# Hash attention and a feed-forward block on one core: hashes taken two pairs ahead, transposes and normalization change places

## The chip, the cores and the metric

The kernel runs on one core of one Trainium2 chip. The metric is the time of the device in microseconds (us), the median of several runs. "PE" is TensorE (PEld its weight loads), "DVE" VectorE, "ACT" ScalarE, "POOL" GpSimd, "SP" SyncE; SPq is SyncE's queue of DMA issues. L432 is line 432 of the kernel.

## What is computed

```python
batch, n_heads, seq, head_dim = (4, 8, 768, 64)           # q, k, v; proj is 64 x 6
q_bits = (np.einsum('bhsd,dk->bhsk', q, proj) > 0)         # the same for k
q_bucket = np.sum(q_bits * powers, axis=-1)                # powers = 1, 2, 4, ... 32
mask = q_bucket[:, :, :, None] == k_bucket[:, :, None, :]
scores = scale * np.matmul(q, k.transpose(0, 1, 3, 2))
scores = np.where(mask, scores, -1000000000.0)
...
attn = np.exp(scores - max) / (sum + 1e-09)
out = np.matmul(attn, v)
# rows of all heads side by side: x is 3072 x 512
h = x @ w_in                                               # 512 x 2048
g = h * (1.0 / (1.0 + np.exp(-1.702 * h)))
y = g @ w_out                                              # 2048 x 512
```

A query sees only the keys whose six hash bits are the same as its own.

## The kernel before

**Pairs of heads.** Attention runs over 16 pairs of heads (`pairs`, L144): two heads of 64 dimensions fill 128 partitions. Pair 0 has a path of its own (`first_pair`), and the loop at L553 takes the pairs 1 to 15. For each pair the kernel needs the keys and the queries turned, so that the dimension lies on the partitions (kT, qT), and a "feature" tile of each (kf, qf), made from the hash bits: the product of features adds a large negative number to each score whose bits differ, so no mask is needed.

**Steps of a pair n**, as functions:
- `fetch` (L317) loads keys or queries, four DMAs of 96 KB each; one buffer for each of the two names. `fetch_v` (L330) loads the values, two DMAs of 192 KB, two buffers.
- `turn` (L388): DVE's transpose L391 of keys or of queries; kT and qT have two buffers each, so kT of pair n+2 lies where kT of pair n lay. `measure` (L393): ACT's sum of squares L398, for a guard.
- `hashed` (L402): PE's matmuls L408 into one bank of PSUM (tag "m"), all four at once in four groups of 32 columns. `featured` (L411): DVE compares the hashes L413 into f (one buffer), and eight small DMAs L420 carry f into the feature tiles, of which there are two sets, for even and odd pairs.
- `scores` (L423): a "phase" for each half c of the queries. For each of six tiles of keys PE adds the product of features and that of keys and queries (L432) into a score tile (pool `sps`, three tiles of two banks), and ACT takes the exponential (L433). The phase with c = 0 is called that on rows, that with c = 1 that on columns.
- `add_low` (L437): POOL adds the first three tiles of exponentials (L440, L441). `add_high` (L443): DVE adds the other three and POOL's sum (L446, L448).
- `values` (L450): PE multiplies by V (L458); c = 0 goes into the bank of pool `aps`, c = 1 into the bank of pool `mps`, the one that hashes use too. `unload` (L466): ACT moves the result into xT (L469, L470).
- `total` (L472): PE sums over the partitions (dn, L479), again four groups of 32 columns. `invert` (L481): DVE turns the sums, takes reciprocals and turns them back (L485 to L494). `norm` (L497): DVE multiplies xT by them (L499).
- `step` and `begin` (L504, L508): six DVE steps and one ACT step (L178 to L198) that convert a chunk of the first weight matrix, one chunk for each pair from 2 on; ACT's step L190 stands ahead of the second unload of the pair in ACT's order.

**What sets the order.** PE, DVE, ACT and POOL are in `manual_schedule` (L72): they do their instructions in the order of the code. SP isn't in it: the order of its DMA issues is found by the framework's scheduler, and each DMA is issued when SP comes to it and its waits are met. So the code of the loop is PE's, DVE's, ACT's and POOL's programme, and a wait in one of these orders holds up all that stands behind it on that engine.

**In the loop before**, pair n has this order on PE: scores on rows, scores on columns, hash of n+1, values of both halves, sums. On DVE: rt of pair n-1, keys of n+1 turned, reciprocals and rs of n-1, queries of n+1 turned, add_high on rows, f of n+1, normalization of n-1, add_high on columns, conversion. In the last pair a guard (`guard`, L516) stands after add_high on rows: DVE reduces the sizes (L518), PE turns them (row, L521), DVE reduces again (L522).

**Feed-forward.** `feed_forward` (L679) follows, with products by seven-multiplication block schemes for both matrices (`hidden`, L700, PE L708; `product_of_halves`, L809, PE L820). `sums_b` of its input (`x_sums`, L514; L219 to L222 on DVE) is spread over the pairs 12 to 15, one step at the end of each. Its first pool of PSUM banks takes the six banks of `sps`, which is closed before (L596). There is a second, slower path behind the guard (L984), which isn't run with this data.

Of the kernel before, what the change touches and what calls it, by code (L numbers as in the profile page):

```python
# [8 lines left out]
F32 = mybir.dt.float32  # L9
# [10 lines left out]
P = 128  # L20
# [18 lines left out]
def kernel(  # L39
# [28 lines left out]
    HS = HT * P  # L68
# [84 lines left out]
    for x in (0x3FFFFFFF, 0xFF800000):  # L153
        m = const.tile([P, 1], U32, name=f"mask_{x:x}")
# [128 lines left out]
    def attention(ff):  # L283
# [4 lines left out]
        with actx:  # L288
# [28 lines left out]
            def fetch(n, name):  # L317

                b, hp = pairs[n]
                x = raws[n, name] = ld.tile([P, S // 32, 32], F32, tag=name, name=name)  # L320
                if (n, name) == (2, "q"):
                    behind(x[:, 0, 0:1])
                src = {"k": k, "q": q}[name]
                for j in range(2):
                    rows = src[b, 2 * hp + j].rearrange("(s p) (a i) -> a p s i", p=32, i=32)
                    for a in range(D // 32):
                        r0 = D * j + 32 * a
                        loader[0].dma_start(out=x[r0 : r0 + 32], in_=rows[a])
# [59 lines left out]
            def turn(n, name):  # L388
                x = raws[n, name]
                xt = xts[n, name] = wk.tile([P, S], F32, tag=f"{name}T", name=f"{name}T")  # L390
                nc.vector.transpose(xt, x.rearrange("p s i -> p (s i)"))  # L391

            def measure(n, name):  # L393

                x = raws.pop((n, name))
                i = 2 * n + "kq".index(name)
                junk = st.tile([P, S], BF16, tag="junk", name="junk", bufs=1)
                nc.scalar.activation(junk, x.rearrange("p s i -> p (s i)"), Act.Square, accum_out=sizes[:, i : i + 1])  # L398
# [3 lines left out]
            def hashed(n):  # L402

                h = dots[n] = mps.tile([P, HS], F32, tag="m", name="hash")
                for i, x in enumerate("kq"):
                    for c in range(2):
                        r0 = D * i + 32 * c
                        nc.tensor.matmul(h[r0 : r0 + 32, :], pf[x], xts[n, x][:, c * HS : (c + 1) * HS],  # L408
                                         start=True, stop=True)

            def featured(n):  # L411
                f = wk.tile([P, HS], BF16, tag="f", name="f", bufs=1)
                nc.vector.tensor_scalar(f, dots.pop(n), above[:, 0:1], weight[:, 0:1], op0=Alu.is_gt, op1=Alu.mult)  # L413
                for c in range(2):
                    for i, x in enumerate("kq"):

                        queue = nc.scalar if (n, x, c) == (1, "q", 0) else nc.sync
                        for j in range(2):
                            r0 = D * i + 32 * c + 2 * NB * j
                            queue.dma_start(out=feats[n % 2][x][D * j : D * j + 2 * NB, c * HS : (c + 1) * HS],  # L420
                                            in_=f[r0 : r0 + 2 * NB, :])

            def scores(n, c, kts):  # L423
                qT, kT, qf, kf = xts[n, "q"], xts[n, "k"], feats[n % 2]["q"], feats[n % 2]["k"]
                cols = slice(c * HS, (c + 1) * HS)
                for kt in kts:
                    ps = sps.tile([P, 2, 512], F32, tag="s", name="ps")
                    keys = slice(kt * P, (kt + 1) * P)
                    for a, m, last in ((kf, qf, False), (kT, qT, True)):
                        for j in range(2):  # L430
                            hs = slice(D * j, D * (j + 1))
                            nc.tensor.matmul(ps[:, j, 0:HS], a[hs, keys], m[hs, cols], start=not last, stop=last)  # L432
                    nc.scalar.activation(es[c][:, kt, :, 0:HS], ps[:, :, 0:HS], Act.Exp, scale=1.0 / D**0.5)  # L433

            accs, avs = {}, {}
# [14 lines left out]
            def values(n, c, kts):  # L450
                if 0 in kts:

                    pool, tag = (mps, "m") if c else (aps, "av")
                    avs[n, c] = pool.tile([P, HS + 1], F32, tag=tag, name="av")
                av, vt = avs[n, c], vts[n]
                for t in kts:
                    for j in range(2):
                        nc.tensor.matmul(av[D * j : D * (j + 1), :], vt[:, t, j, :], es[c][:, t, j, :],  # L458
                                         start=(t == 0), stop=(t == T - 1))
# [6 lines left out]
            def unload(n, c):  # L466
                av = avs.pop((n, c))
                vs = st.tile([P, 1], F32, tag="vs", name="vs")
                nc.scalar.copy(vs, av[:, HS : HS + 1])  # L469
                nc.scalar.activation(x_of(n)[:, c * GT : (c + 1) * GT, :], av[:, 0:HS].rearrange("p (t s) -> p t s", t=GT), Act.Identity, bias=vs[:, 0:1])  # L470

            def total(n):  # L472

                dn = accs[n] = aps.tile([P, HS], F32, tag="av", name="dn")
                for c in range(2):
                    acc = accs.pop((n, c))
                    for j in range(2):
                        r0 = D * j + 32 * c
                        nc.tensor.matmul(dn[r0 : r0 + 32, :], ones[:, 0:32], acc[:, j, :], start=True, stop=True)  # L479

            def invert(n):  # L481


                rt = st.tile([P, HS // 32, 32], F32, tag="rt", name="rt", bufs=1)
                nc.vector.transpose(rt.rearrange("p s i -> p (s i)"), accs.pop(n))  # L485
                yield
                r = st.tile([P, 2, HS // 32], F32, tag="r", name="r")
                nc.vector.reciprocal(r, rt[:, :, 0].unsqueeze(1).to_broadcast([P, 2, HS // 32]))
                for r0 in range(0, P, 32):
                    c = r0 // 32 % 2  # L490
                    r1 = r0 + 32 - 64 * c
                    nc.vector.reciprocal(r[r1 : r1 + 32, c], rt[r0 : r0 + 32, :, 0])
                rs = accs[n] = st.tile([P, S], F32, tag="rs", name="rs", bufs=1)
                nc.vector.transpose(rs.rearrange("p (s i) -> p s i", i=32),  # L494
                                    r.rearrange("p c s -> p (c s)").unsqueeze(2).to_broadcast([P, S // 32, 32]))

            def norm(n):  # L497
                x, rs = x_of(n), accs.pop(n)
                nc.vector.tensor_tensor(x, x, rs.rearrange("p (t s) -> p t s", t=T), op=Alu.mult)  # L499
# [4 lines left out]
            def step(n, count=1):  # L504
                for _ in range(count):
                    next(conv.get(n, iter(())), None)
# [40 lines left out]
            fetch(2, "q")  # L547
            fetch_v(1)
            scores(0, 1, high)
            values(0, 1, low)  # L550
            values(0, 1, high)
            unload(0, 1)
            for n in range(1, last + 1):  # L553
                scores(n, 0, every)
                add_low(n, 0)
                if n == 1:
                    add_high(0, 1)
                    turn(2, "k")
                    total(0)
                inverted = invert(n - 1)  # L560
                next(inverted)
                if 1 < n < last:
                    turn(n + 1, "k")
                whole(inverted)
                scores(n, 1, every)
                add_low(n, 1)
                if n < last:
                    turn(n + 1, "q")
                add_high(n, 0)
                if n < last:  # L570
                    hashed(n + 1)
                    featured(n + 1)
                    for x in "kq":
                        measure(n + 1, x)
                else:
                    guard(0)
                    guard(1)
                norm(n - 1)
                add_high(n, 1)
                values(n, 0, every)  # L580
                unload(n, 0)
                step(n, 6)
                values(n, 1, every)
                unload(n, 1)
                total(n)
                if n + 2 <= last:
                    for x in "kq":
                        fetch(n + 2, x)
                if n < last:
                    fetch_v(n + 1)  # L590
                    begin(n + 1)
                if n > last - len(x_sums):
                    x_sums[n - last - 1]()
# [378 lines left out]
    def whole(steps):  # L972
        for _ in steps:
            pass
# [46 lines left out]
```

## Time and profile before

| | |
|---|---|
| median of 3 runs | 877.33 us (876.5 to 877.67) |
| profiled execution: time, span | 876.77 us, 875.0 us |
| granted clock of TensorE | 0.997 |
| attention, to the first feed-forward product | 322.8 us |
| a pair from 2 on | 19.28 us (71.11 to 90.39) |

Share of the chain of work that ended last, by line:

```profile
PE 90%; DVE 6%; SPq 1%; DMA 1%; issue 1%; ACT 0%; ACTq 0%; DVEq 0%
```

The page gives busy time by engine and by group of instructions, the timeline the instructions of an engine in order of time. A row of the timeline has the start, the duration, the engine, the line, the operation, the tile that is written and those that are read, and the count; at its end, in brackets, stands the idle time before it and what ended that. Rows of like instructions are merged. A stretch of the span is given with its busy us for each engine, the granted clock, the share of the DMA engines and the GB/s that they moved. For a DMA the row on SPq is that of its issue.

### The profile page before, as it was taken

To read this page: it belongs to the slowest core of one execution; us is meant where nothing else is said; L and a number is where in the kernel's file an instruction comes from. 1 tells how busy PE (TensorE), PEld (TensorE's weight loads), DVE (VectorE), ACT (ScalarE), POOL (GpSimd) and SP (SyncE) were. 2 spreads that over 40 slices of the span, in tenths; PEclk is the share of its full clock that TensorE was granted. 3 is DMA by queue.
4 is the path that set the end of the run, shared out by engine and by line. 5 is a ranking of instruction groups with operands and counts; after the bars stand their busy time and mean duration, and the time that the engine had idled before them with its cause. 6 is when DMAs were issued, how large, how long until landed. Compare 5 with 4: busy or idle time off the path is not lost.

```text
span 875.0 us, 11818 instructions
## 1 busy us (share of the span) xinstructions
PE 861.9 (99%) x4077; PEld 502.7 (57%) x4077; DVE 719.6 (82%) x1020; ACT 310.2 (35%) x519; POOL 321.3 (37%) x275
## 2 busy tenths in 40 slices
PE   9999999999999999999999999999999999999995
PEld 4444445444444444444444444444888888888884
DVE  4579999988999997788777787888888977897785
ACT  5756567777666743222233222332000000000000
POOL 4243334334333475665443344659903100000000
PEclk9999999999999999999999999999999999999998
DMA  5334456644445304555455645575844685467524
GB/s 133 59 59 85 83 97 106 119 87 83 84 83 93 73 25 145 204 205 204 166 188 190 214 168 200 193 251 168 308 160 163 199 244 198 166 203 241 193 97 99
DMA packets 169155, 131.99 MB, mean 151 GB/s; under 512 B 123616, under 2 KB 138112, under 8 KB 163712
## 3 DMA queue, kind: packets, MB, share of 16 engines
q1 hardware_dynamic: 166528, 129.70, 51.5%
q10 hardware_dynamic: 2560, 1.46, 0.7%
q8 instruction: 34, 0.56, 0.3%
q14 instruction: 33, 0.27, 0.1%
HBM read 79.69 MB, written 50.33 MB: 149 GB/s over the span
## 4 chain that ended last, share of the span: by engine, by line
PE 90%; DVE 6%; SPq 1%; DMA 1%; issue 1%; ACT 0%; ACTq 0%; DVEq 0%
PE product L708 33%; PE product L820 27%; PE ps L432 16%; PE av L458 12%; PE dn L479 1%; PE hash L408 1%; DVE acc L448 1%; DVE acc L446 1%; DVE xT L824 1%; SPq L420 1%; DVE y L800 1%; DVE xT L499 1%; DMA pj<-in_proj_dram 0%; DMA k<-in_k_dram 0%; DVE t_x L221 0%
## 5 line engine op out<-in xcount | busy, mean ns | idle before, releaser
L432 PE MATMUL ps<-qT,kT 64*128 64x384 f32 x768 | 155.1, 483 | 0.0
L433 ACT ACTIVATE e<-ps 128x768 f32<-128x768 f32 x192 | 149.0, 813 | 15.7 <-PE ps L432 13.7
L708 PE MATMUL product<-xT,w_in_sb 128*128 128x512 f32 x288 | 135.5, 593 | 0.0
L458 PE MATMUL av<-e,v 128*64 128x385 f32 x768 | 128.2, 488 | 0.0
L440 POOL TENSOR_TENSOR acc<-e 128x768 f32<-128x768 f32 x32 | 50.4, 1575 | 192.2 <-ACT e L433 113.4
L716 ACT ACTIVATE c<-c 128x512 f32<-128x512 f32 x72 | 45.3, 630 | 186.7 <-issue 78.6
L458 PEld LDWEIGHTS av<-e,v 128*64 128x64 f32 x768 | 53.9, 136 | 72.8 <-issue 71.9
L708 PEld LDWEIGHTS product<-xT,w_in_sb 128*128 128x128 f32 x288 | 54.7, 190 | 68.9 <-issue 64.4
L708 PE MATMUL product<-t_x,s_in 128*128 128x512 f32 x192 | 90.3, 592 | 0.0
L432 PEld LDWEIGHTS ps<-qT,kT 64*128 64x128 f32 x768 | 68.3, 188 | 36.1 <-issue 35.2
L219 POOL TENSOR_TENSOR v<-c,u 128x512 f32<-128x512 f32 x24 | 34.2, 1423 | 122.8 <-ACT c L716 122.8
L833 ACT COPY u<-product 128x256 f32<-128x256 f32 x21 | 7.8, 372 | 172.1 <-PE product L820 138.9
L441 POOL TENSOR_TENSOR acc<-acc,e 128x768 f32<-128x768 f32 x32 | 64.1, 2002 | 2.5
L432 PE MATMUL ps<-qf,kf 64*128 64x384 bf16 x384 | 63.1, 324 | 0.1
L708 PEld LDWEIGHTS product<-t_x,s_in 128*128 128x128 f32 x192 | 36.6, 190 | 45.9 <-issue 43.2
L446 DVE SCALAR_TENSOR_TENSOR acc<-e 128x768 f32<-128x768 f32 x32 | 52.1, 1628 | 5.1 <-ACT e L433 5.1
L708 PE MATMUL product<-xT,s_in 128*128 128x512 f32 x96 | 45.1, 592 | 0.0
L708 PE MATMUL product<-t_x,w_in_sb 128*128 128x512 f32 x96 | 45.1, 592 | 0.0
L432 PEld LDWEIGHTS <-kf 64*128 64x128 bf16 x384 | 20.4, 94 | 36.1 <-issue 12.4
L820 PE MATMUL product<-raw_g,xT 128*128 128x256 f32 x152 | 35.1, 379 | 0.0
L448 DVE TENSOR_TENSOR acc<-acc,e 128x768 f32<-128x768 f32 x32 | 31.0, 969 | 3.8 <-ACT e L433 0.5
L448 DVE TENSOR_TENSOR acc<-acc,acc 128x768 f32<-128x768 f32 x32 | 31.0, 969 | 3.3
(207 smaller groups left out, 1496.4 us busy)
## 6 DMA issues: line engine op xcount, KB each, us to landing
raw_g<-g_dram SPq DMA_DIRECT2D x22, 1024.0 KB
s_in<-g_dram SPq DMA_DIRECT2D x20, 1024.0 KB
g_dram<-c SPq DMA_DIRECT2D x72, 256.0 KB
g_dram<-t SPq DMA_DIRECT2D x48, 256.0 KB
raw<-in_moe_w_in_dram SPq DMA_DIRECT2D x16, 512.0 KB
raw<-in_moe_w_out_dram SPq DMA_DIRECT2D x16, 512.0 KB
v<-in_v_dram SPq DMA_DIRECT2D x32, 192.0 KB
g_dram<-u SPq DMA_DIRECT2D x24, 256.0 KB
```

Of the source, the lines that this page charges most:

```text
L219: return [lambda: eng.tensor_tensor(t1, b12, b11, op=Alu.subtract), lambda: eng.tensor_tensor(b12, b22, b12, op=Alu.subtract), lambda: eng ...
L408: nc.tensor.matmul(h[r0 : r0 + 32, :], pf[x], xts[n, x][:, c * HS : (c + 1) * HS], start=True, stop=True)
L432: nc.tensor.matmul(ps[:, j, 0:HS], a[hs, keys], m[hs, cols], start=not last, stop=last)
L433: nc.scalar.activation(es[c][:, kt, :, 0:HS], ps[:, :, 0:HS], Act.Exp, scale=1.0 / D**0.5)
L440: nc.gpsimd.tensor_tensor(acc, es[c][:, 0, :, 0:HS], es[c][:, 1, :, 0:HS], op=Alu.add)
L441: nc.gpsimd.tensor_tensor(acc, acc, es[c][:, 2, :, 0:HS], op=Alu.add)
L446: nc.vector.scalar_tensor_tensor(acc, e[0], T * TINY, e[1], op0=Alu.add, op1=Alu.add)
L448: nc.vector.tensor_tensor(acc, acc, x, op=Alu.add)
L458: nc.tensor.matmul(av[D * j : D * (j + 1), :], vt[:, t, j, :], es[c][:, t, j, :], start=(t == 0), stop=(t == T - 1))
L708: nc.tensor.matmul(ps, wq[LEFT[i]][:, kc, :], xq[RIGHT[i]][:, kc, :], start=(kc == 0), stop=(kc == K2 - 1))
L716: nc.scalar.activation(c, c, Act.Gelu_apprx_sigmoid)
L820: nc.tensor.matmul(ps, wq[LEFT[i]][:, c, :], gq[RIGHT[i]][:, c, :], start=(c == 0), stop=(c == F4 - 1))
```

## The change

- `measure` keeps the raw tile in its table (no instruction changes).
- `values` of the half c = 1 goes into one of the three score tiles of `sps` instead of the bank of `mps`.
- Hashes are made two pairs ahead. In pair n the keys and queries of pair n+2 are turned and measured after add_high on rows; `hashed(n + 2)` stands after both halves of the values and before the sums, and `featured(n + 2)` after the sums. The fetch is three pairs ahead. Pair 1 makes up for the start: it also turns, measures, hashes and features pair 2.
- `norm(n - 1)` follows `invert(n - 1)` at once, before add_high on rows.

So in pair n PE's order is now: scores on rows, scores on columns, values, hash of n+2, sums. DVE's: rt, reciprocals, rs and normalization of n-1, add_high on rows, keys and queries of n+2 turned, add_high on columns, conversion, f of n+2. The numbers of instructions are the same.

```diff
-                x = raws.pop((n, name))
+                x = raws[n, name]
...
-                    pool, tag = (mps, "m") if c else (aps, "av")
-                    avs[n, c] = pool.tile([P, HS + 1], F32, tag=tag, name="av")
+                    if c:
+                        avs[n, c] = sps.tile([P, 2, 512], F32, tag="s", name="av1")[:, 0, 0 : HS + 1]
+                    else:
+                        avs[n, c] = aps.tile([P, HS + 1], F32, tag="av", name="av")
...
             scores(0, 1, high)
+            measure(2, "k")
             values(0, 1, low)
             values(0, 1, high)
             unload(0, 1)
             for n in range(1, last + 1):
+
                 scores(n, 0, every)
                 add_low(n, 0)
                 if n == 1:
                     add_high(0, 1)
-                    turn(2, "k")
+                    for x in "kq":
+                        turn(2, x)
+                    fetch(3, "k")
                     total(0)
-                inverted = invert(n - 1)
-                next(inverted)
-                if 1 < n < last:
-                    turn(n + 1, "k")
-                whole(inverted)
+                    measure(2, "q")
+                    fetch(3, "q")
+                whole(invert(n - 1))
+                norm(n - 1)
                 scores(n, 1, every)
                 add_low(n, 1)
-                if n < last:
-                    turn(n + 1, "q")
                 add_high(n, 0)
-                if n < last:
-                    hashed(n + 1)
-                    featured(n + 1)
+                if n == 1:
+                    hashed(2)
+                    featured(2)
+                if n + 2 <= last:
                     for x in "kq":
-                        measure(n + 1, x)
-                else:
+                        turn(n + 2, x)
+                        measure(n + 2, x)
+                if n == last:
                     guard(0)
                     guard(1)
-                norm(n - 1)
                 add_high(n, 1)
                 values(n, 0, every)
                 unload(n, 0)
                 step(n, 6)
+                if n + 3 <= last:
+                    for x in "kq":
+                        fetch(n + 3, x)
                 values(n, 1, every)
                 unload(n, 1)
+                if n + 2 <= last:
+                    hashed(n + 2)
                 total(n)
                 if n + 2 <= last:
-                    for x in "kq":
-                        fetch(n + 2, x)
+                    featured(n + 2)
                 if n < last:
                     fetch_v(n + 1)
                     begin(n + 1)
```

## The prediction, made before the changed kernel was run

> **What bounds the kernel now.** I read the busy shares first, then stretches of the span, then TensorE row by row where it is not full, then SyncE's queue.
>
> ```profile
> PE 861.9 (99%) x4077; PEld 502.7 (57%) x4077; DVE 719.6 (82%) x1020; ACT 310.2 (35%) x519; POOL 321.3 (37%) x275
> ```
>
> ```profile
> 51.00:273.00 222.00, 222.00 (x1570) 106.07 (x1572) 201.51 (x265) 151.23 (x242) 80.97 (x46) 1.00 0.53 95
> 273.00:313.00 40.00, 39.30 (x278) 18.27 (x274) 38.12 (x48) 27.50 (x44) 15.71 (x8) 1.00 0.29 61
> 313.00:323.00 10.00, 9.19 (x58) 3.91 (x59) 9.39 (x9) 0.90 (x3) 8.96 (x6) 1.00 0.00 0
> 323.00:612.00 289.00, 289.00 (x676) 128.43 (x676) 231.13 (x308) 84.34 (x141) 160.98 (x132) 1.00 0.54 188
> ```
>
> The columns of the stretches are length, then busy us of PE, PEld, DVE, ACT and POOL. From 51 to 273 us, pairs 2 to 13, TensorE has no idle time at all; neither has it in the feed-forward part. DVE, at 201.5 of 222, is a close second: it decides nothing now, but has little room. So the change can shorten the kernel only where PE idles or loses time between matmuls, and it lengthens it wherever PE has to wait anew. PE's rows show both places:
>
> ```profile
> 50.99 0.84 PE L479 MATMUL dn<-acc,ones 128*32 128x384 f32 x4 [0.31 <-DVE acc L448]
> ...
> 80.10 0.81 PE L432 MATMUL ps<-qT,kT 64*128 64x384 f32 x4
> 80.84 0.52 PE L408 MATMUL hash<-kT,pf_k 128*32 128x384 f32 x2
> ...
> 81.19 0.49 PE L408 MATMUL hash<-kT,pf_k 128*32 128x384 f32 x2
> ...
> 81.62 0.87 PE L458 MATMUL av<-e,v 128*64 128x385 f32 x4
> ...
> 313.81 0.27 PE L521 MATMUL row<-ident,largest 128*1 128x128 f32 x1 [1.52 <-DVE largest L518]
> ```
>
> Two waits are left: 0.31 us before dn of pair 1 and 1.52 us before the guard's row in pair 15. And each change of shape costs a little: hash's second pass starts at 81.19, lasts about 0.32 (the pass distance inside av is 0.32), yet av starts at 81.62, 0.11 later than it could.
>
> SyncE's queue around pairs 1 and 2, and the DMA traffic behind its last entry (last two columns: DMA share, GB/s):
>
> ```profile
> 44.09 1.52 SPq L420 DMA_DIRECT2D kf<-f  x2
> ...
> 48.68 1.47 SPq L420 DMA_DIRECT2D qf<-f  x2
> 50.26 2.16 SPq L328 DMA_DIRECT2D k<-in_k_dram  x4
> 52.52 3.38 SPq L328 DMA_DIRECT2D q<-in_q_dram  x4
> 55.99 1.17 SPq L340 DMA_DIRECT2D v<-in_v_dram  x2
> ```
>
> ```profile
> 59.00:59.50 0.50, 0.50 (x6) 0.35 (x4) 0.50 (x2) 0.44 (x2) 0.00 (x0) 1.00 0.65 103
> 59.50:60.00 0.50, 0.50 (x6) 0.24 (x4) 0.50 (x2) 0.50 (x1) 0.00 (x0) 1.00 0.01 2
> ```
>
> Eight transfers of features take 6.06 us of issue (44.09 to 50.15), keys and queries 2.2 each, V 1.0 to 1.2; V's issue ends at 57.16 and its bytes stop at about 59.4: V lands some 2.2 us after its issue.
>
> [...] normalization L499 takes 2.00 us beside GpSimd's additions and 0.96 at 338.56 us alone, L446 2.43 against 0.92. [...]
>
> **The change, part by part** (T is the start of a pair's scores; a pair lasts 19.28 us: scores 9.80, hash 0.78, values 7.92, sums 0.78).
>
> *Hash beside the sums.* PE's order scores, hash, values, sums becomes scores, values, hash, sums: same matmuls, same number of shape changes, but hash and sums have one shape. If the 0.11 us shrinks to the 0.03 that hash loses between its own passes, that is 0.08 for each of 13 pairs (hashes 3 to 15): 1.0 us gained. Bounds 0 and 13 x 0.11 = 1.4.
>
> *DVE's order.* The two transposes (0.98 and 0.94) leave the phase on rows for the one on columns; normalization goes the other way; f moves behind the conversion. Transposes keep 0.98 beside GpSimd's additions (75.33). For pair n I get: f to T+1.1, rt, the five reciprocals and rs to 3.9, normalization beside GpSimd's first sums (2.7 to 6.5) 2.0, to 5.8, add_high on rows to 9.3, then transposes from 9.9, since the buffer they write is read by this pair's scores to 9.8; to 11.8; add_high on columns to 15.7, conversion to 19.9. It fits, with 0.3 us to spare, and acc is ready 2.7 us ahead of the sums. In pair 1 add_high ends near 49.5 instead of 50.95: the 0.31 us goes. In pair 14 there is nothing left to turn or hash, 2.6 us less, so the guard's reduction, at T+11.15 in before (313.58 less 302.43), comes near T+9.7, when the scores end: 1.42 of 1.52 us goes.
>
> *The second half of the values in a score bank.* av1 takes the place of one of three score tiles, so the third score tile of the next pair waits for ScalarE's unload (L469, L470). Behind conversion L190 this ends at T-0.7 and is needed at T+1.6: hidden, and if DVE ran 2.5 us later, it would show. In the end it does: the first feed-forward product takes the same banks, and in the built program it has a new wait on ScalarE. There unload stands behind L190, and that behind DVE's L182. Before, that unload ended at 324.96, 2.2 us after the first product. By my count L182 ends at T+17.9, unload at T+19.4, and PE is ready at T+18.8: 0.65 us lost (bounds 0 and 2.2). Behind PE all of the feed-forward part is queued, so it counts in full.
>
> *SyncE's queue.* The order there is the scheduler's and not written by hand; the built program shows it. Before, V of pair 2 was out by 34.8 us, right behind V of pair 1 (32.03, 2.76 us for the four). Now it stands behind keys and queries of 3, features of 2, keys and queries of 4 and features of 3. With the durations of before: features of 2 to 50.15; keys and queries, at the same place as those of before, to 55.9; features of 3 (ready by 53: hash 3 ends at 50.6 on PE, and f, one buffer, waits for the features of 2 to land, near 52.3) 6.1 to 62.0; V 1.0 to 63.1; landed 65.3. PE wants it when the scores of pair 2 end: 61.63 in before, less 0.31 and 0.08, 61.24. **A wait of 4.1 us**, PE's whole stream behind it. Bounds: without the long issue of 3.38 (2.2 instead) 2.9; with another delay like that of 0.7 (issues of 2.17 instead of 1.47 at 87.53) 4.8. Nothing covers it: the next instruction of PE that doesn't need V stands behind it.
>
> V of pair 3 stands behind the features of 4. f of 4 starts 0.93 us after hash 4 starts (274.60 less 273.67), ending at T+0.14; 6.1 to 6.8 us of issue, V 1.0, landing 2.2: T+9.5 to T+10.2, wanted at T+9.8. I take 0.3 us (bounds 0 and 0.6). From V of pair 4 on it goes out one pair ahead: no wait. Keys and queries go out two pairs ahead, with more than a phase to spare.
>
> *ScalarE.* measure moves; its two squares (0.83 each) stay ahead of the unload of the values. Nothing.
>
> *Sum:* -1.0 -0.31 -1.42 +0.65 +4.1 +0.3 = **+2.3 us**. Against the profiled execution, 876.77 us (span 875.0, 1.8 around it), that is 879.1. The median of the runs, 877.33, is 0.56 above it; I put the sum on the median: 879.6.
>
> **Rivals.**
> - *The short wait, not slower.* SyncE issues without the long 3.38, V lands at 64.1 and the wait is 2.9; V of pair 3 is in time (0); the join gives its upper 1.4. Sum: -1.4 -0.31 -1.42 +0.65 +2.9 = +0.4, 877.7. For it: most issues of keys and queries take 2.16. Against it: the long one stood at just this place. It decides from a wait below 3.5 us.
> - *No wait worth the name.* If V arrived within 1 us of its need, the gains would stand: -2.7 +0.65 +1.0 = -1.1, and with the upper join and no wait at the banks -2.1: 875.2. Against it: the queue's 0.72 us for each of eight feature transfers, which no row undercuts.
> - *DVE becomes the bound.* If GpSimd's additions slow both L446 and the normalization in each pair (1.5 us more than before), DVE needs 18.7 + 1.5 = 20.2 us a pair against 19.2; over 11 pairs it falls behind, the first 3 us are free, and half of the rest already gives +3 on top of my sum: 882.6. For it: 201.5 of 222 us; against: GpSimd's second pair of additions now falls beside transposes, which it doesn't slow.
>
> **How the numbers follow.** Measurements of this kernel can tell about 0.2% (1.75 us) from no change, so the borders are 875.58 and 879.08. My forecast with the long wait: 0.48, all but slower by its size. Short wait: 0.38, within. No wait: 0.07, faster. DVE: 0.07, slower. So faster 0.07, same 0.38, slower 0.55. The range goes from 876.6 (short wait with the low bounds of the other terms gives 877.1; half of the no-wait case is taken in) to 882.6 (long wait 4.8, no join, 2.2 at the feed-forward start, or the DVE case); below it lies most of 0.07, above it 0.05. The forecast's own range is 878.9 to 881.5.
>
> **What would show it.** One wait of PE on V's transfer of 3 to 5 us near 61 us, and a small one or none in pair 3; none from pair 4 on, with pairs of 19.2 us instead of 19.28. Row's wait below 0.3 us; a wait of the first product on ScalarE's xT of 0.3 to 2. DVE's kT waiting for PE in each pair. I'd be wrong if PE waits recur in every pair (banks or sums: DVE), or if V of pair 2 lands before 62.

## The result, and the profile after

The changed kernel takes 882.16 us (median of 6 runs, 881.62 to 884.44) against 877.26 for the kernel before in the same session (876.5 to 877.67): 4.9 us more, a ratio of 1.0062 with a 95% interval of 1.0049 to 1.0075. Run again later it took 881.63 (881.03 to 883.12) against 877.05, ratio 1.0058 (1.0044 to 1.0071). The forecast was +2.3 us: the sign and the main place were right, the size was less than half of what came. The profiled execution of the changed kernel took 883.48 us, one of its slowest; it lies 6.71 above the profiled execution of before, and the sums below are made against it.

From the page of the changed kernel, the busy line and the row of PE's granted clock over the 40 slices:

```profile
PE 863.4 (98%) x4077; PEld 504.3 (57%) x4077; DVE 722.4 (82%) x1020; ACT 313.3 (36%) x519; POOL 313.9 (36%) x275
...
PEclk9998999999999999999999999999999999999998
```

PE has lost a point of its share, and the clock, full throughout attention before, has a dip in the fourth slice (66 to 88 us). The first and the last of the stretches of the prediction, now of the changed kernel:

```profile
51.00:273.00 222.00, 216.84 (x1520) 102.96 (x1518) 200.48 (x253) 146.90 (x233) 72.07 (x44) 0.98 0.54 92
...
323.00:612.00 289.00, 288.17 (x701) 127.48 (x697) 232.34 (x305) 83.35 (x140) 159.98 (x131) 1.00 0.52 183
```

PE was busy for all 222 us of the first stretch; now 5.16 are idle, and the mean clock is 0.98. DVE is as busy as it was (200.5 against 201.5): it has not become the bound. PE's waits, summed over the trace of the changed kernel (what waited, what ended it, us in total, times, longest):

```profile
PE av L460 <- DMA v<-in_v_dram: 5.2, 1, 5.2
PE av L460 <- ACT e L433: 1.6, 1, 1.6
...
PE product L716 <- ACT xT L472: 0.8, 1, 0.8
```

The waits of before (row 1.5, dn 0.3) are gone, and three new ones have come. PE's timeline of the changed kernel has them in their places:

```profile
27.88 4.10 PE L460 MATMUL av<-e,v 128*64 128x385 f32 x24 [1.65 <-ACT e L433]
...
51.96 0.83 PE L481 MATMUL dn<-acc,ones 128*32 128x384 f32 x8
...
67.75 11.53 PE L460 MATMUL av<-e,v 128*64 128x385 f32 x48 [5.16 <-DMA v<-in_v_dram]
...
320.35 0.27 PE L523 MATMUL row<-ident,largest 128*1 128x128 f32 x1
...
330.15 1.99 PE L716 MATMUL product<-xT,w_in_sb 128*128 128x512 f32 x4 [0.83 <-ACT xT L472]
```

The first is in pair 0. The second is the foreseen one, V of pair 2; but the values that follow it take 11.53 us in place of 7.99. There are two reasons. The first is in the stretches of 1 us around it (the third column from the end is the clock):

```profile
66.00:67.00 1.00, 0.00 (x0) 0.00 (x0) 0.90 (x2) 0.00 (x0) 0.00 (x0) 0.95 1.03 234
67.00:68.00 1.00, 0.25 (x1) 0.28 (x2) 0.90 (x2) 0.00 (x0) 0.00 (x0) 0.50 1.33 248
...
72.00:73.00 1.00, 1.00 (x6) 0.42 (x4) 0.44 (x1) 0.00 (x0) 0.00 (x0) 0.50 1.05 96
73.00:74.00 1.00, 1.00 (x8) 0.48 (x6) 0.00 (x0) 0.00 (x0) 0.00 (x0) 0.64 0.00 0
```

While PE stood idle (from 62.58), its clock was halved, at 66.9; it came back at 73.7, 6 us after the matmuls had begun again: six matmuls in the microsecond from 72, at a clock of 0.50, where the run with the filler below has ten at 1.00. The second reason is V itself. It comes as two DMAs, one for each head, and the weight loads of the values (PEld) show that the second lands 1.2 us after the first:

```profile
67.72 0.29 PEld L460 LDWEIGHTS av<-e,v 128*64 128x64 f32 x2 [5.75 <-DVE acc L446]
68.95 0.34 PEld L460 LDWEIGHTS av<-e,v 128*64 128x64 f32 x4 [0.94 <-DMA v<-in_v_dram]
```

SyncE's queue of the changed kernel, up to V of pair 2:

```profile
45.94 1.58 SPq L420 DMA_DIRECT2D kf<-f  x2
...
52.34 2.79 SPq L328 DMA_DIRECT2D k<-in_k_dram  x4
55.23 2.38 SPq L328 DMA_DIRECT2D q<-in_q_dram  x4
57.74 1.59 SPq L420 DMA_DIRECT2D kf<-f  x2
...
64.50 1.10 SPq L340 DMA_DIRECT2D v<-in_v_dram  x2
```

This is the order that the prediction worked from, shifted: the features of pair 2, with which it begins, start 1.85 us later than in before (45.94 against 44.09).

Where the time went, from the starts of groups in PE's timeline of both profiled executions:

| stretch | before | after | difference |
|---|---|---|---|
| start of the span to the second half of the values of pair 0 | 26.43 | 27.88 | +1.45 |
| from there to the scores of pair 2 | 25.34 | 24.84 | -0.50 |
| pair 2 | 19.28 | 27.92 | +8.64 |
| pair 3 | 19.27 | 19.82 | +0.55 |
| pairs 4 to 13 | 192.84 | 191.40 | -1.44 |
| pair 14 (its hash has gone to pair 1) | 19.27 | 18.50 | -0.77 |
| pair 15 to the first feed-forward product | 20.28 | 19.79 | -0.49 |
| from there to the end of the span | 552.29 | 551.55 | -0.74 |

### The profile page after: what moved, and what is told of

It is laid out like the page before. It is cut to its first block, busy times and chain, and to the rows that moved or that the text cites. A ratio compares the mean times of both kernels' runs of the same rounds, so it can differ in the third digit from the quotient of the medians.

```text
span 881.7 us, 11940 instructions
## 1 busy us (share of the span) xinstructions
PE 863.4 (98%) x4077; PEld 504.3 (57%) x4077; DVE 722.4 (82%) x1020; ACT 313.3 (36%) x519; POOL 313.9 (36%) x275
## 4 chain that ended last, share of the span: by engine, by line
PE 91%; DVE 5%; DMA 1%; issue 1%; POOL 1%; ACTq 0%; SPq 0%; ACT 0%; DVEq 0%; POOLq 0%
PE product L716 33%; PE product L828 27%; PE ps L432 15%; PE av L460 13%; PE hash L408 1%; PE dn L481 1%; DVE acc L448 1%; DVE xT L832 1%; DMA v<-in_v_dram 1%; DVE y L808 1%; DMA q<-in_q_dram 0%; DVE acc L446 0%; DVE xT L501 0%; PE hash L373 0%; ACTq L420 0%
## 5 line engine op out<-in xcount | busy, mean ns | idle before, releaser
L433 ACT ACTIVATE e<-ps 128x768 f32<-128x768 f32 x192 | 151.1, 812 | 29.2 <-PE ps L432 26.7
L460 PE MATMUL av<-e,v 128*64 128x385 f32 x768 | 132.5, 496 | 6.8 <-DMA v<-in_v_dram 5.2
L460 PEld LDWEIGHTS av<-e,v 128*64 128x64 f32 x768 | 56.0, 138 | 80.8 <-issue 71.2
L219 POOL TENSOR_TENSOR v<-c,u 128x512 f32<-128x512 f32 x24 | 34.2, 1425 | 123.8 <-ACT c L724 123.8
L441 POOL TENSOR_TENSOR acc<-acc,e 128x768 f32<-128x768 f32 x32 | 56.8, 1776 | 2.5
L448 DVE TENSOR_TENSOR acc<-acc,e 128x768 f32<-128x768 f32 x32 | 34.4, 1075 | 3.3
```

Source lines behind the costliest of these rows:

```text
L219: return [lambda: eng.tensor_tensor(t1, b12, b11, op=Alu.subtract), lambda: eng.tensor_tensor(b12, b22, b12, op=Alu.subtract), lambda: eng ...
L441: nc.gpsimd.tensor_tensor(acc, acc, es[c][:, 2, :, 0:HS], op=Alu.add)
L448: nc.vector.tensor_tensor(acc, acc, x, op=Alu.add)
```

## The experiments

The theory after this reading: the loss has three separate places (V of pair 2 with the clock behind it, the score bank in pair 0, the unload ahead of the first product), and the join is a small gain in every pair. The rivals: DVE's or ACT's new order is at fault, or the slow values come from the memory traffic and not from PE's idleness. Each ratio below is against the kernel before in the same session (876.83 to 877.05 us).

**V fetched a pair's length earlier.** Edit to the changed kernel:

```diff
+                if n < last:
+                    fetch_v(n + 1)
                 scores(n, 0, every)
...
                 if n < last:
-                    fetch_v(n + 1)
                     begin(n + 1)
```

> The changed kernel, with the values of pair n+1 fetched at the beginning of pair n; in the built program V of pair 2 goes out right behind V of pair 1 as in the kernel before, V of pair 3 one pair ahead. Theory (V behind the features costs the wait and, through it, the clock): no wait of TensorE on V in pairs 2 and 3, TensorE's clock at 1.00 throughout pair 2, pair 2 lasts 19.15 us instead of 27.91; 5.2 + 3.6 + 0.7 = 9.5 us less span than the profiled changed kernel, so about 872 of span and 874 of time. Rival A (the clock falls for another reason): the waits go, but the values of pair 2 still take 11.5 us: 5.9 us less. Rival B (the transfers of V are late for lack of bandwidth, wherever they stand): the wait stays above 2 us.

Measured: 874.18 us (873.8 to 874.89, 11 runs) against 876.83 for before in that session, ratio 0.9972 (0.9963 to 0.9981). That is 8.0 below the changed kernel, and faster than before. The values of pair 2 in its timeline:

```profile
62.78 7.99 PE L460 MATMUL av<-e,v 128*64 128x385 f32 x48
```

No wait, full speed, and pair 2 lasts 19.14 us. Pair 3 lasts 19.14 too, so its 0.55 us were V as well (in the changed kernel its first matmuls start in time, at 90.43, and V's second DMA holds up the next weight load for 0.50 us, to 91.12). The place of V in the queue accounts for all that pairs 2 and 3 lost; DVE's and ACT's new order is untouched here and costs nothing in them. The other two waits stay (1.64 and 0.84).

**PE kept busy during the wait.** 24 matmuls on a tile of zeros, 128x512 in bf16, ahead of the values of pair 2; the result doesn't use them (the trace has 23 of them):

```diff
+                if n == 2:
+                    w = mps.tile([P, 512], F32, tag="m", name="filler")
+                    for _ in range(24):
+                        nc.tensor.matmul(w, idle[:, 0:P], idle, start=True, stop=True)
                 values(n, 0, every)
```

> The changed kernel, with 24 matmuls more on TensorE in pair 2 between scores and values, on a tile of zeros into the hash bank, which nobody reads [...]: they fill the wait for V, which stays as late as it was. Theory [...]: with TensorE busy the clock stays at 1.00, the values of pair 2 take 7.9 us instead of 11.5, V is waited for as before: 3.6 us less than the changed kernel. Rival (the slow values come from transfers or from something else beside them, keys and queries of pair 5 being fetched at that time): they still take over 10 us, and nothing is gained.

Measured: 881.71 us (881.57 to 882.26, 4 runs), ratio 1.006 (1.0043 to 1.0077). Its timeline, and then one stretch of it:

```profile
62.68 5.35 PE L587 MATMUL filler<-idle 128*128 128x512 bf16 x23
68.12 0.83 PE L460 MATMUL av<-e,v 128*64 128x385 f32 x2
69.31 7.98 PE L460 MATMUL av<-e,v 128*64 128x385 f32 x46 [0.37 <-DMA v<-in_v_dram]
```

```profile
70.00:71.00 1.00, 1.00 (x10) 0.44 (x8) 0.97 (x2) 0.00 (x0) 0.00 (x0) 1.00 1.50 142
```

The clock stays at 1.00, and from 69.31 on the values run at full speed, beside the same DMA traffic (share 1.50, 142 GB/s) beside which they had crept at half clock: in the changed kernel the stretch from 70 to 71 has 1.57 and 144. So here it was in PE's idleness that the clock was halved, and not by the traffic. The 1.2 us between the first two matmuls of the values and the others remain at full clock: they are V's second DMA, which lands 3.3 us after the end of the issue (66.02) here and 3.35 us after it (65.60) in the changed kernel. So of the 3.5 us by which the values of pair 2 were longer there, 2.3 are the clock: from the landing of V's second half they took 10.3 us to their end, and 8.0 here.

My expectation of 3.6 us less failed. The median is 0.4 us below the first session of the changed kernel and 0.1 above the second, too little to give the filler a size. V was issued 0.42 us later in this trace; and the changed kernel itself doesn't lose 2.3 us at the clock each time, as the run after next shows.

**A shorter wait.** Does the clock stay at 1.00 if the wait for V is shorter? The queries of pair 4 are issued behind V of pair 2, in pair 1 alone:

```diff
-                    for x in "kq":
+                    for x in "k" if n == 1 else "kq":
                         fetch(n + 3, x)
...
                     fetch_v(n + 1)
+                    if n == 1:
+                        fetch(4, "q")
```

> The changed kernel with one fetch moved: the queries of pair 4 are issued behind V of pair 2 instead of ahead of the features of pair 3. The queue reaches V some 2.4 us earlier, so the wait for V shrinks from 5.2 to about 2.8 us but stays. Theory: [...] here it stays at 1.00, the values of pair 2 take 7.9 us instead of 11.5, and both together give 6.0 us: 876.2 us against 882.2 of the changed kernel. Rival: the slower values belong to any wait for V, or to the traffic of the DMA engines beside them; then the values take over 11 us again and only the 2.4 us of the shorter wait are won: 879.8 us.

Measured: 881.88 us (880.92 to 882.34, 5 runs), ratio 1.005 (1.0036 to 1.0063). My expectation failed. PE's row, and two stretches:

```profile
66.66 11.11 PE L460 MATMUL av<-e,v 128*64 128x385 f32 x48 [3.71 <-DMA v<-in_v_dram]
```

```profile
64.00:65.00 1.00, 0.00 (x0) 0.00 (x0) 0.46 (x1) 0.64 (x2) 1.00 (x1) 1.00 0.14 35
65.00:66.00 1.00, 0.00 (x0) 0.00 (x0) 0.00 (x0) 0.00 (x0) 0.92 (x2) 0.57 1.11 253
```

The wait shrank by 1.5 us only (the keys' issue took 3.48 in place of 2.79), and the clock fell at 65.14 by the mean of the second stretch, 2.2 us after PE's last matmul at 62.95. So it did not stay at 1.00: a fall after 4.3 us in one trace had been taken for a limit. What sets the place of the fall is open after this run; my guess was that it isn't tied to PE's last matmul.

**The changed kernel once more.** If that is so, the loss must differ from execution to execution. The same kernel again:

> The changed kernel itself once more, for its spread. In the three traces in which TensorE waited for V of pair 2 for 3.7 to 5.2 us its clock fell 2.2, 3.6 and 4.3 us after its last matmul and came back 6.8 us after it fell, each time. Theory: [...] the place of the fall, and with it what the values of pair 2 lose (up to 3.6 us), differs from execution to execution: times between 880.5 and 884.5 us, median about 882, and in the new trace values of 9 to 11.6 us whose slow stretch is 3.4 or 6.8 us long. Rival: a fixed delay after the last matmul, with differences from other causes; then the fall comes 4.3 us into the wait again.

Measured: 881.63 us (881.03 to 883.12, 5 runs). PE's row and two stretches of the new trace:

```profile
67.37 9.96 PE L460 MATMUL av<-e,v 128*64 128x385 f32 x48 [5.13 <-DVE acc L448]
```

```profile
66.50:67.00 0.50, 0.00 (x0) 0.00 (x0) 0.50 (x1) 0.00 (x0) 0.04 (x1) 0.70 1.17 252
70.00:70.50 0.50, 0.50 (x6) 0.32 (x4) 0.47 (x1) 0.00 (x0) 0.00 (x0) 0.89 1.58 143
```

The same wait (5.13 us) but 9.96 us of values and not 11.53: the clock fell at 66.70 and was back at 70.11, by the means of these two stretches: after 3.4 us and not 6.8. (The trace ascribes this wait to DVE's addition, which the values don't read; V's issue ended at 65.27, 2.1 us before, as in the other traces, so I take it for V's.)

The clock fell in a wait for V in five traces: the changed kernel twice, the shorter wait, and two runs below (pair 0 in the hash bank, and V of pair 2 alone put forward). The fall came 4.3, 4.5, 2.2, 3.6 and 3.4 us after PE's last matmul, so a fixed delay, the rival, is out; the half clock then lasted 6.8, 3.4, 6.8, 6.8 and 3.4 us. The half clock of the second trace of the changed kernel, and, for a wait without a fall, a stretch of the score bank alone (below), whose wait of 2.23 us ends at 327.22:

```profile
66.70:70.11 3.41, 2.74 (x8) 0.95 (x10) 3.24 (x5) 0.00 (x0) 0.00 (x0) 0.50 1.47 165
325.39:328.81 3.42, 1.59 (x4) 0.87 (x5) 3.32 (x4) 1.29 (x3) 3.26 (x4) 1.00 0.00 0
```

What decides between 3.4 and 6.8 us is not shown: one execution of the changed kernel had 6.8, another 3.4.

**V of pair 2 alone put forward.** Keys and queries of pair 4 both go behind V of pair 2; SP's queue then has V ahead of the features of pair 3 as well:

```diff
-                if n + 3 <= last:
+                if n + 3 <= last and n > 1:
                     for x in "kq":
                         fetch(n + 3, x)
...
                     fetch_v(n + 1)
+                    if n == 1:
+                        fetch(4, "k")
+                        fetch(4, "q")
```

> The changed kernel with keys and queries of pair 4 (in pair 1 alone) issued behind V of pair 2; V of pair 2 then goes out ahead of the features of pair 3 as well, and every other pair keeps its queue. Theory: the loss of pair 2 is the place of its V in the queue and nothing else, so its wait and its slow values go: no wait in pair 2, values of 7.9 us, while the small loss at V of pair 3 (0.7 us) and the 0.84 us at the first feed-forward product stay: 874.9 us. Rival: with more in the queue behind V, keys, queries or V of pair 3 are late in their turn: a wait of over 2 us in pair 3, 877 us or more.

Measured: 882.66 us (882.03 to 883.73, 5 runs), ratio 1.0067 (1.0053 to 1.008). The rival was right. PE's timeline:

```profile
62.53 7.99 PE L460 MATMUL av<-e,v 128*64 128x385 f32 x48
...
73.69 0.84 PE L481 MATMUL dn<-acc,ones 128*32 128x384 f32 x4 [1.49 <-DVE acc L448]
87.79 10.29 PE L460 MATMUL av<-e,v 128*64 128x385 f32 x48 [3.15 <-DMA v<-in_v_dram]
```

Pair 2 has its V in time; its sums then wait for DVE, whose transposes wait 4.09 us for the keys and 1.66 for the queries that were put back, and pair 3 has V's wait and the slow clock (from 88.00 to 91.42). The loss has only moved on by a pair. So the cause is wider than one V's place. As I read it, the queue has more to issue in pairs 1 to 3 than there is time for, and what stands last in it is late. With V ahead in every pair it pays off: V of pair 2 then goes out at 32 to 35 us together with V of pair 1, as in the kernel before, and the queue, which has nothing to issue from 41.3 to 46.2 us in that trace, has room for it there.

**The second half of the values of pair 0 in the hash bank**, and, the other way round, **the score bank alone in the kernel before**. The two edits, to the changed kernel and to the kernel before:

```diff
                     if c and n == 0:
+                        avs[n, c] = mps.tile([P, HS + 1], F32, tag="m", name="av")
+                    elif c:
                         avs[n, c] = sps.tile([P, 2, 512], F32, tag="s", name="av1")[:, 0, 0 : HS + 1]
```

```diff
-                    pool, tag = (mps, "m") if c else (aps, "av")
-                    avs[n, c] = pool.tile([P, HS + 1], F32, tag=tag, name="av")
+                    if c:
+                        avs[n, c] = sps.tile([P, 2, 512], F32, tag="s", name="av1")[:, 0, 0 : HS + 1]
+                    else:
+                        avs[n, c] = aps.tile([P, HS + 1], F32, tag="av", name="av")
```

> The changed kernel, with the second half of the values of pair 0 alone in the bank that hashes use, as before. Theory (that half waits in pair 0 for the exponential that frees its score bank): the wait of 1.65 us in pair 0 goes and pair 1 starts 1.7 us earlier; but SyncE's queue from pair 1 on, which is then started earlier by the same, moves too, so the wait for V in pair 2 stays at some 5 us: 1.7 us less than the changed kernel. Rival A: the wait is for V or for the features (transfers), and stays. Rival B: the queue of SyncE doesn't move, so the wait for V grows by what pair 0 gains: no change.

> The kernel before with one part of the change alone: the second half of the values goes into a score bank instead of the hash bank. Theory: three places pay. Pair 0 waits 1.7 us for an exponential; pairs 1 to 15 pay nothing, or tenths, where ScalarE's unload behind the conversion comes later than the third score tile (T+1.6; before it ended at T+1.2 to T+1.7); and the first feed-forward product waits for the last unload, which ended 2.2 us after it in the kernel before. Sum 3.9 us more than before, up to 6 with tenths in the pairs. Rival (the bank costs nothing, the score tiles have room): within 0.5 us of before.

Measured: 881.13 us (880.68 to 881.37, 4 runs) for the first, 1.0 below the changed kernel; 881.63 us (880.9 to 882.39, 4 runs), ratio 1.0059 (1.0042 to 1.0075), for the second. The second's waits of PE:

```profile
PE product L710 <- ACT xT L472: 2.2, 1, 2.2
PE av L460 <- ACT e L433: 1.6, 1, 1.6
```

The edit of the bank alone makes the kernel 4.8 us slower: 1.64 in pair 0, 2.23 at the first product, and some 0.5 that its profiled execution lost in the opening (its hash of pair 0 starts at 8.68 us, in before at 8.17; the two traces of the changed kernel have 7.90 and 7.55, so this scatters); the last 0.4 is not placed. Its pairs still last 19.28, so the bank costs nothing within them, as predicted. The first kernel's trace has the values of pair 0 at once, at 26.57; V of pair 2 is still late by 4.93 us with the clock halved (11.13 us of values), so that wait isn't a consequence of the one in pair 0. Its gain is 1.0 against the changed kernel's first session and 0.5 against its second, not 1.65; with a half clock of 3.4 us in one execution of the changed kernel and 6.8 in another, these medians can't size it, and the sum of all three edits below does.

**The join undone.** The early V, with the hash of two pairs ahead put between the halves of the values:

```diff
                 unload(n, 0)
...
+                if n + 2 <= last:
+                    hashed(n + 2)
                 values(n, 1, every)
                 unload(n, 1)
-                if n + 2 <= last:
-                    hashed(n + 2)
                 total(n)
```

> The changed kernel with V fetched early, and the hash of two pairs ahead put between the two halves of the values instead of beside the sums: same matmuls, same buffers, the join undone. Theory: the join is worth 0.13 us a pair, so a pair of the rows from 4 to 13 lasts 19.27 instead of 19.14 us, dn takes 0.78 instead of 0.65, and 13 hashes give 1.7 us: 875.9 against 874.18 with the join. Rival: the shorter pairs come from something else in the new order (the banks, DVE's order); then dn or the values stay as they are and the time is within 0.4 us of 874.2.

Measured: 878.57 us (877.6 to 879.2, 21 runs), ratio 1.0015 (1.0009 to 1.0022): 4.4 more than with the join, where I had said 1.7. Pair 3 in its timeline:

```profile
71.54 0.85 PE L481 MATMUL dn<-acc,ones 128*32 128x384 f32 x8
82.12 4.10 PE L460 MATMUL av<-e,v 128*64 128x385 f32 x24
86.15 0.52 PE L408 MATMUL hash<-kT,pf_k 128*32 128x384 f32 x2
...
86.94 4.10 PE L460 MATMUL av<-e,v 128*64 128x385 f32 x24
90.97 0.85 PE L481 MATMUL dn<-acc,ones 128*32 128x384 f32 x8
```

A pair lasts 19.43 us (90.97 less 71.54). I had miscounted: the edit doesn't only part hash and sums, it cuts the values in two as well. A pair changes its form of matmul 3 times with the join (19.14 us), 4 times in before (19.28) and 5 times here (19.43): 0.14 to 0.15 us for each change, and the join takes away one. Thirteen times two changes give 3.8 us. The profiled executions differ by 3.5 and the medians by 4.4 (this one is the fastest of the 21), so the price of a change is read from the pairs, and what the medians have above it is not explained.

**The unload ahead of the conversion, in the last pair alone**, with the early V:

```diff
                 unload(n, 0)
-                step(n, 6)
+                if n < last:
+                    step(n, 6)
...
                 unload(n, 1)
+                if n == last:
+                    step(n, 6)
```

> The changed kernel with V fetched early, and in the last pair alone the unload of the values ahead of the conversion step on ScalarE. Theory: the first feed-forward product waits for that unload because it stands behind the conversion; moved ahead, the wait of 0.84 us goes and nothing else changes: 873.3 us against 874.18. Rival: the conversion is then late and the sums, or the next steps that use it, wait as long instead: 874.2 us, with the 0.8 us found before dn or behind the first product.

Measured: 873.32 us (873.16 to 874.05, 5 runs), ratio 0.9954 (0.994 to 0.9968): 0.86 below the early V alone, as expected. The first product follows dn directly:

```profile
319.83 0.85 PE L481 MATMUL dn<-acc,ones 128*32 128x384 f32 x8
320.77 1.98 PE L720 MATMUL product<-xT,w_in_sb 128*128 128x512 f32 x4
```

**All three together**: early V, pair 0 in the hash bank, the unload first in the last pair.

> The changed kernel with three edits: V of the next pair is fetched at the beginning of a pair, the second half of the values of pair 0 goes to the hash bank, and in the last pair the unload of the values stands ahead of the conversion step on ScalarE. Theory: the three waits are separate and add up. Against the run with the early fetch of V alone (874.18) the wait of 1.6 us in pair 0 and the wait of 0.84 us at the first feed-forward product both go: 871.7 us, with no wait of TensorE over 0.4 us between 30 and 330 us. Rival: the time that is won in pair 0 turns into waits for V or for features in pairs 1 and 2, since the DMA queue doesn't move with TensorE: 873.3 us or more, with the wait of pair 0 gone and a new one by 75 us.

Measured: 871.79 us (871.01 to 872.08, 5 runs) against 876.96 for before, ratio 0.9935 (0.9922 to 0.9949): 5.2 us faster than before and 10.4 faster than the changed kernel. The list of PE's waits has one line left, at the start of the kernel:

```profile
PE warm L359 <- DVE idle L76: 1.2, 1, 1.2
```

The three places add up (874.18 less 1.64 less 0.84 is 871.7), so nothing that was won turned into a new wait.

## Why the prediction fell short, step by step

| step of the prediction | predicted | measured in the profiled execution |
|---|---|---|
| join of hash and sums, 13 times | -1.0 (0 to -1.4) | -1.8 (13 x 0.14) |
| sums of pair 1 | -0.31 | -1.13 |
| guard's row | -1.42 | -1.39 |
| first product waits for the unload | +0.65 (0 to 2.2) | +0.9 |
| wait for V of pair 2 | +4.1 (2.9 to 4.8) | +5.2 |
| V of pair 3 (its second DMA) | +0.3 (0 to 0.6) | +0.7 |
| score bank in pair 0 | "hidden" | +1.7 |
| slow values behind the wait for V: half clock, V's second DMA | not in the sum | +3.5 (+2.0 in the second trace) |
| start of the span, and what follows the last product | not in the sum | -0.3, -0.7 |
| sum | +2.3 | +6.7 |

Two steps failed: the cost of the wait for V was taken to end with the wait, and the score bank was taken to be hidden everywhere. Step by step:

- *The wait for V: right mechanism, a term too small.* The forecast had V landing at 65.3 and PE ready at 61.24; they were 67.75 and 62.58. The hash of pair 2, 1.44 late (42.59, in before 41.15), moves both ends. The 1.1 us between them come from the queue: the features of pair 2 start 3.35 us after that hash and not 2.94, and the two sets of features take 6.28 and 6.76 us (45.94 to 52.22, 57.74 to 64.50) and not 6.06 and 6.1. The landing was right for V's first DMA, 2.15 us after the end of the issue against 2.2, and wrong for the second, 3.35: the 2.2 had been read where nothing stood behind V in the queue, and here the next keys and queries did. That they delay it is not shown.
- *"Nothing covers it"*, and the cost was taken to end with the wait. That step failed. PE's clock fell to 0.50 while it waited, and the work behind the wait paid. No wait of before shows that: the longest in its loop, 1.52 us, lies in a stretch with a clock of 1.00 (313 to 323 us). An estimate from the traces of the changed kernel: 3.4 us at a clock of 0.50, if full of matmuls, cost half their length, 1.7 us. Here the values took 2.0 and 3.5 us longer (9.89 and 11.45 from their start to the hash's, less 7.92). About 0.7 and 2.3 of it are the clock (8.7 and 10.3 us from the landing of V's second half to the end, against 8.0 in the run with the filler), the rest, 1.2 to 1.3, is that second half.
- *"Behind conversion L190 this ends at T-0.7 and is needed at T+1.6: hidden".* True for the pairs of the loop, and they show no wait. But pair 0 has code of its own: there three score tiles have just been written when the values ask for one, and ACT, which issues two feature DMAs itself just before, only starts their exponentials at 26.92:

```profile
24.54 2.34 ACTq L420 DMA_DIRECT2D qf<-f  x2
26.92 2.22 ACT L433 ACTIVATE e<-ps 128x768 f32<-128x768 f32 x3 [2.80 <-PE ps L432]
```

  One sentence of the prediction looked only at the third score tile of the next pair, not at the tile that the values themselves ask for. Cost: 1.7 us.
- *Sums of pair 1.* The bracket of 0.31 us was taken for the whole loss. The rows showed more: dn in two halves from 49.85, the scores of pair 2 at 51.77, 1.92 us where one dn takes 0.79. The wait also broke the overlap of the halves.
- *The join.* The bound of 1.4 counted only the change into the values. The change into dn falls away too (dn starts 0.67 after the hash, and the scores 0.76 after dn in place of 0.78): 0.14, outside the bound. That the join gives nothing, the lower bound, did not come true.
- *Row and first product* came as worked out. L182 ended at T+18.4 (forecast 17.9), the unload at T+19.7 (19.4).
- *DVE the bound, short wait, no wait*: none came; pairs 4 to 13 last 19.14 us without a wait of PE. Two slips there changed nothing: half of the 8 us that DVE would fall behind is 4 and not 3, and the normalization at 338.56 was not alone: GpSimd's L222 started 0.11 us after it and took 1.98 us, where L219 to L221 just before took 1.27.

The losses were put too low by 7.0 us (1.7 and 3.5 left out, 1.1, 0.4 and 0.25 too small), the gains by 2.6 (0.8, 0.8 and 1.0 at the two ends): 4.4 us net in the profiled executions, 2.6 in the medians. The 0.7 us at the end lies behind DVE's last transpose, in the last stores and the end of the program: from PE's last matmul to the end of the span it is 9.4 us in before, 9.5 with the score bank alone, and 8.5 to 8.6 in each run of the changed order. So it belongs to the new order; why stays open.

## What to carry to other kernels

A wait on TensorE can cost more than its length: the waits of 3.1 to 5.2 us here had 3.4 or 6.8 us at half clock from the fall on, one of 2.2 us had none, and the same kernel had 6.8 us in one execution and 3.4 in another. Price it so, and remove the wait first: filling it kept the clock here, but won next to nothing in time. When a tensor comes in several DMAs, price the landing of the last. When a result moves to another buffer, check every place that asks for that buffer, the prologue's own code first, and when work is moved a step earlier, add up the issue time of the whole DMA queue around the first pairs: what stands last there is what gets late, and moving one transfer forward only passes the lateness on unless a gap takes it. A bracket in the timeline shows the wait, not the overlap that the wait broke; take the loss from start to start.

## What the runs showed of the hardware

- In five traces PE's clock fell to 0.50 in a wait for V of 3.1 to 5.2 us, 2.2 to 4.5 us after the last matmul ahead of the wait, and was back 3.4 or 6.8 us after the fall. It stayed at 1.00 where matmuls filled the wait, and in a wait of 2.23 us at the first product (the score bank alone).
- V, two DMAs of 192 KB issued one after the other: in the two traces of the changed kernel and in that with the filler the values could start on the first 2.1 to 2.2 us after the end of the issue of both, and on the second 3.3 to 3.4 us after it.
- A change of the form of matmul (128x385 with 64 columns, 128x384 in four groups of 32 columns, the scores' pairs) costs 0.14 to 0.15 us by the length of the pairs: 19.14, 19.28 and 19.43 us a pair with 3, 4 and 5 changes.
